# Mixture of experts behind a decayed linear attention: the building of the token lists is put in another order

## The chip, the cores and the metric

One Trainium2 chip, one of its cores. The metric is device time in microseconds (us) of one execution. The engines are named as the profile names them: PE (matrix products; PEld its weight loads), DVE (VectorE), ACT (ScalarE), POOL (GpSimd), SP (SyncE, which issues most transfers). Every engine works through its own instructions in program order and waits for other engines by semaphores.

## The reference

```python
# attention: 4 batches, 8 heads, 768 tokens, head size 64
for t in range(S):
    state = gamma * state + outer(k[t], v[t])
    y[t] = scale * q[t] @ state
x = y as (3072 tokens, 512)
# experts: 4 groups of 4, each token goes to one expert
g = argmax(x @ w_group);  e = argmax(x @ w_expert[g])
out[token] = softmax_g * softmax_e * (relu(x @ w1[g, e]) @ w2[g, e])
```

A token's expert, and the weight that its result is multiplied by, come from x, so they are known only once the attention has reached that token.

## The kernel before

**Attention.** `attention` takes 12 steps `i`, each of 128 tokens of two batches (256 tokens, `u` = 0, 1). A step on PE is: `score_mm` of the next step (L235), `state_out` (L286), `value_out` (L299), `state_mm` (L261), `logits_mm` of the step before (L319: the 20 router logits), transposes of keys (L220) and of x (L345), `select_mm` (L332). On DVE it is: `score_mask` (four instructions of L247 to each step, a pair to each `u`: pf <- sh) and `out_x` (a pair of L311: the x products, xt <- op). A matmul that reuses the bank of a score waits until L247 has read it. x goes to DRAM (`xd`), from where the experts gather their tokens.

**Lists.** Four chunks of 128 tokens are a batch (`BATCHES`, six of them). `route` is a generator; `route_steps` runs it on to its next "wait". For one batch it issues on DVE the argmaxes down to the one-hot of the expert, `oh` (L384 to L402); `weights` (six instructions L413 to L426 that end with the reciprocal `wt`, then four that split `wt` into three bf16 pieces of `pc`, L428 to L434); rank matmuls on PE (L441, L443); the sums down to the slot `sf` of each token (L451 to L460). For batches 3 to 5 (`soon`) the weights come ahead of the ranks, or right behind them for the last one. Then `spread`: `places` (three small instructions L483 to L485: tile `y` and place `p` of the slot), `entries` (on DVE the tile's marks `sel`, L503; on POOL their product with the pieces, `ent`, 128x640, L505) and `marks` (the one-hots `hot` of the place, 128x512 on DVE, L492). `tally` multiplies hot with ent on PE (L526) and adds the result to `lists` (L531). In steps 4, 6, 8 and 10 weights and `spread` stand on DVE between the two pairs of L247; `tally` is at the end of the step, in step 10 ahead of `value_out`.

**First units.** `ua` is expert 0's first 128 tokens (taken from the first 16 chunks), `ub` the rest of expert 0 (up to 108), `va` expert 1 (`us[0]`). Behind the attention `run` interleaves ua's matmuls (`layers`, L834 with hidden halves f0 to f3, then L869) with batch 5: ranks, `late_spread` (a second one-hot of the slots beyond 128, L555 on DVE, `latep` L550 on POOL), `late_ids` (L563) which gives ub's tokens, the gather of ub, the last spread and tally, the gather of va. `own_cols` gives column counts that PE loads into shape registers (`shape`, L801). `order` sorts the experts by size. hl (the low part of h, L842, for ua L1306 from a list `held`) is made on DVE.

**Weights.** Each expert's four 1 MB tiles `wf` are split in eight parts by `wsplit`: the high part on ACT (L745), the low one `wl` on DVE (L747, 128x1024). Expert 0's low parts are made on POOL beside the attention (128x512). Of va's, parts 0 and 1 stand on DVE ahead of ub's first hl, parts 2 to 5 one behind each of the four hl, and parts 6 and 7 go to POOL:

```python
if i == 7:
    for k in (6, 7):
        self.wsplit(va, k, eng=nc.gpsimd, high=False)
    self.wload(us[1], 3)
```

Then follow xbl of va's two token tiles (L812 on DVE), which va's first matmul needs. From there on the 15 units run one after another.

Of the kernel before, what the change touches and what calls it, by code (L numbers as in the profile page):

```python
# [22 lines left out]
P = 128  # L23
# [83 lines left out]
class Kernel:  # L107
# [251 lines left out]
    def route(self, i):  # L359
# [50 lines left out]
        soon = c0 + n >= EARLY  # L410

        def weights():
# [15 lines left out]
            V.tensor_copy(pc[:, :, 2], wt)  # L428
            yield 1
            V.tensor_tensor(wt, wt, pc[:, :, 2], ALU.subtract)  # L430
            yield 1
            V.tensor_copy(pc[:, :, 3], wt)
            yield 1
            V.tensor_tensor(pc[:, :, 4], wt, pc[:, :, 3], ALU.subtract)  # L434
            yield 1
# [25 lines left out]
        yield 1  # L461
        if end:
            self.late_spread()
            yield "late"
# [9 lines left out]
        if not end:  # L474
            self.spread(i)

    def places(self, b):

        c0, n = BATCHES[b]
        sf = self.sf[:, c0:c0 + n]  # L480
        p = self.rp.tile([P, BM], F32, name="place")
        y = self.rp.tile([P, BM], F32, name="tile")
        self.nc.vector.tensor_scalar(y, sf, 0.5 - P / 2, ROUND, ALU.add, ALU.add)  # L483
        self.nc.vector.tensor_scalar(y, y, ROUND, None, ALU.subtract)
        self.nc.vector.tensor_tensor(p, sf, y, ALU.subtract)  # L485
        return p, y
# [8 lines left out]
    def entries(self, b, y, eng):  # L495

        c0, n = BATCHES[b]
        buf = self.bp.tile([P, 4, P], F32, name="yT", bufs=1).rearrange("p d t -> p (d t)").bitcast(BF16)
        m = BM * NL
        ent = buf[:, 0:m * PIECES].rearrange("p (c l w) -> p c l w", c=BM, l=NL)  # L500
        sel = buf[:, m * PIECES:m * PIECES + m].rearrange("p (c l) -> p c l", c=BM)
        tb = self.rest[:, C_TB:C_TB + NL].unsqueeze(1).broadcast_to([P, BM, NL])
        self.nc.vector.tensor_tensor(sel, tb, y.unsqueeze(2).broadcast_to([P, BM, NL]), ALU.is_equal)  # L503
        pc = self.pc[:, c0:c0 + n].unsqueeze(2).broadcast_to([P, BM, NL, PIECES])
        eng.tensor_tensor(ent, sel.unsqueeze(3).broadcast_to([P, BM, NL, PIECES]), pc, ALU.mult)  # L505
        return ent

    def spread(self, b):

        p, y = self.places(b)  # L510
        ent = self.entries(b, y, self.nc.gpsimd)
        self.spreads.append((self.marks(p), ent))
# [55 lines left out]
    def own_cols(self):  # L568
# [5 lines left out]
        V.tensor_scalar(self.late_cols, f, float(LATE), None, ALU.min)  # L574
        self.own = self.rp.tile([1, 2], I32, name="ocols")
        for i, w in enumerate((P, LATE)):
            f = self.rp.tile([1, 1], F32, name="fcols%d" % i)
            V.tensor_scalar(f, nb[0:1, 1:2], float(-CAP - i * P), 1.0, ALU.add, ALU.max)
            V.tensor_scalar(self.own[:, i:i + 1], f, float(w if i else P + LATE), None, ALU.min)
# [483 lines left out]
    def attention(self, extra, beside):  # L1063
# [27 lines left out]
        for i in range(NS2):  # L1091
# [7 lines left out]
            if i:  # L1099
                if i > 2:  # L1100
                    self.outs(i)
                if i > 1:
                    scores(i + 1, 0)
                if i % 2 and not last:
                    self.select_late()
# [15 lines left out]
            if i == 10:  # L1121
                self.tally()
            beside(i, 5)
# [7 lines left out]
            self.state_copy(i)  # L1131
            beside(i, 4)
# [3 lines left out]
            if i < 2:  # L1136
                scores(i + 1, 0)
                scores(i + 1, 1)
            if last:
# [24 lines left out]
            if last:  # L1164
                self.route_steps(99)
            if i % 2:
# [5 lines left out]
            if i in (4, 6, 8):  # L1172
                self.tally()
# [19 lines left out]
    def run(self):  # L1193
        tc, nc = self.tc, self.nc
        with ExitStack() as ctx:
# [45 lines left out]
            def beside(i, place):  # L1241
# [14 lines left out]
                if place == 2:  # L1256
                    if last:
                        self.xtrans(ua, 'big', (0,), low=False)
                        self.wsplit(va, 0, low=False)
# [18 lines left out]
            self.trans_mm(last, self.yp)  # L1278
            self.wsplit(va, 1, low=False)
# [10 lines left out]
            first(2)  # L1290
            self.wsplit(va, 2, low=False)
            next(route)
            first(2)
            while next(route) != "late":
                pass
            p, y = self.places(len(BATCHES) - 1)
            ub["mt"] = self.pairs()
            self.late_ids(ub["mt"])
            ent = self.entries(len(BATCHES) - 1, y, nc.gpsimd)
            self.gather(ub)  # L1300
            for _ in route:
                pass
            self.spreads.append((self.marks(p), ent))
# [4 lines left out]
            self.own_cols()  # L1308
            for k in range(2):
                nc.scalar.activation(self.xg[1][:, k], self.one, AF.Copy, scale=0.0)  # L1310
            self.wsplit(va, 3, low=False)
            self.steps.append(self.order())
            self.route_steps(99)
            assert not self.steps
            pick(1)
            pick(2)
            for i, k in enumerate(self.first):
                if i == 0:
                    self.shape(ub, 5, 0, self.late_cols)
                if i == 1:  # L1320
# [15 lines left out]
            for i, k in enumerate(self.layers(ub)):  # L1336
                if i == 0:
                    self.counts()
                if i < 8 and i % 2:
                    self.wsplit(va, 4 + i // 2, low=False)  # L1340
                    self.wsplit(va, 2 + i // 2, high=False)
                    if i % 4 == 3:
# [88 lines left out]
```

## Time and profile before

| | |
|---|---|
| median of 3 runs | 421.93 us (420.22 to 423.2) |
| the profiled execution | 422.39 us, of which the span of its instructions 420.5 |
| busy: PE, DVE, ACT, POOL | 398.8, 301.8, 224.6, 161.0 us |
| mean granted clock of PE | 0.974 of 2.4 GHz |

Times of rows are microseconds from the span's start in the profiled execution, which is the one that sums are made against. A row of a timeline has start, length, engine, line, operation, output <- inputs, count and, in brackets, the idle time before it and what ended it.

### The profile page before, as it was taken

How to read it: one execution, taken by the hardware profiler on the slowest of the kernel's cores; microseconds unless marked ns; L12 is line 12 of the kernel's file. 1: busy time of each engine (PE TensorE's matmuls, PEld its weight loads, DVE VectorE, ACT ScalarE, POOL GpSimd, SP SyncE). 2: the span in 40 equal slices, each digit the busy share in tenths (PEclk: the TensorE clock that was granted, in tenths of full speed). 3: DMA queues.
4: the chain of work that ended last, by engine and by line, in shares of the span. 5: the costliest groups of instructions: out<-in, count | busy, mean ns of one | idle time of the engine just before them, and what ended most of it. 6: DMA issues, size and time to landing. Idle time of an engine off the chain costs nothing.

```text
span 420.5 us, 13852 instructions
## 1 busy us (share of the span) xinstructions
PE 398.8 (95%) x5805; PEld 331.5 (79%) x5837; DVE 301.8 (72%) x525; ACT 224.6 (53%) x342; POOL 161.0 (38%) x130
## 2 busy tenths in 40 slices
PE   9999979989979599999999999999999999999992
PEld 5889868868758487868788797978979879788792
DVE  4576794965799666988676877768778788697630
ACT  2335334531646066556565665766667667667620
POOL 4543647436437500622233450614405225052011
PEclk9999998996999789999999999999999999999997
DMA  7999998882875836778686978789887898888001
GB/s 264 352 320 359 348 327 282 272 284 85 270 223 182 334 125 231 252 248 263 232 258 240 301 267 288 256 296 284 296 306 279 282 327 279 295 302 294 13 35 36
DMA packets 39507, 107.13 MB, mean 255 GB/s; under 512 B 12116, under 2 KB 12244, under 8 KB 32276
## 3 DMA queue, kind: packets, MB, share of 16 engines
q1 hardware_dynamic: 29760, 93.57, 65.0%
q0 software_dynamic: 9536, 12.63, 8.8%
q8 instruction: 47, 0.77, 0.7%
q14 instruction: 16, 0.13, 0.1%
q10 hardware_dynamic: 148, 0.03, 0.1%
HBM read 94.18 MB, written 13.20 MB: 255 GB/s over the span
## 4 chain that ended last, share of the span: by engine, by line
PE 49%; issue 29%; DVE 11%; POOL 9%; POOLq 0%; ACT 0%; DVEq 0%; ACTq 0%
PE hps L834 14%; PE yps L869 6%; PE yps L916 5%; POOL out L993 5%; PE op L299 4%; PE sh L235 4%; PE yps L919 3%; POOL xg L769 3%; PE op L286 2%; DVE wl L747 2%; PE sh L345 2%; PE stp L261 2%; PE tpx L787 1%; PE sh L220 1%; PE log L332 1%
## 5 line engine op out<-in xcount | busy, mean ns | idle before, releaser
L747 DVE TENSOR_TENSOR wl<-wf,wh 128x1024 bf16<-128x1024 f32 x118 | 147.8, 1261 | 38.1 <-ACT wh L745 37.8
L745 ACT ACTIVATE wh<-wf 128x1024 f16<-128x1024 f32 (+1 forms) x136 | 133.8, 1001 | 0.0
L834 PE MATMUL hps<-xbl,wh 128*128 128x128 f16 (+16 forms) x544 | 130.1, 251 | 2.0 <-DVE xbl L812 1.4
L834 PE MATMUL hps<-xbh,wh 128*128 128x0 bf16 x544 | 127.2, 243 | 0.0
L834 PE MATMUL hps<-xbh,wl 128*128 128x0 bf16 x544 | 127.1, 243 | 0.0
L993 POOL DMA_INDIRECT out<-yo,mt x30 | 39.4, 1315 | 163.5 <-ACT yo L975 125.8
L834 PEld LDWEIGHTS <-wh 128*128 128x128 f16 x1088 | 96.0, 99 | 3.5 <-issue 2.5
L919 PEld LDWEIGHTS <-wh 128*128 128x128 f16 x768 | 47.1, 97 | 22.9
L839 ACT ACTIVATE hh<-hps 128x256 bf16<-128x256 f32 (+16 forms) x68 | 34.2, 503 | 48.1 <-PE hps L834 47.7
L769 POOL DMA_INDIRECT xg<-xd,mt x30 | 52.5, 1750 | 10.9 <-issue 2.9
L834 PEld LDWEIGHTS <-wl 128*128 128x128 bf16 x544 | 53.7, 99 | 1.2
L247 DVE TENSOR_TENSOR pf<-sh,tri 128x512 f32<-128x512 f32 x48 | 30.7, 685 | 23.1 <-PE op L299 9.7
L842 DVE SCALAR_TENSOR_TENSOR hl<-hps,hh 128x216 f16<-128x216 f32 (+15 forms) x64 | 36.8, 574 | 9.4 <-ACT hh L839 9.0
L789 ACT ACTIVATE xbh<-tpx 128x512 bf16<-128x512 f32 (+14 forms) x32 | 16.7, 523 | 46.4 <-PE tpx L787 46.4
L916 PE MATMUL yps<-wh,hh 128*128 128x512 f16 x96 | 36.4, 379 | 0.0
L916 PE MATMUL yps<-wh,hl 128*128 128x512 f16 x96 | 36.4, 379 | 0.0
L916 PE MATMUL yps<-wl,hh 128*128 128x512 bf16 x96 | 36.3, 378 | 0.0
L192 POOL TENSOR_TENSOR vs<-lv,cst 128x512 f32<-128x512 f32 x24 | 24.6, 1042 | 22.6 <-DMA lv<-qkv 10.0
L919 PEld LDWEIGHTS <-wl 128*128 128x128 bf16 x384 | 24.2, 97 | 11.4
L812 DVE TENSOR_TENSOR xbl<-tpx,xbh 128x512 f16<-128x512 f32 (+14 forms) x32 | 19.0, 597 | 18.7 <-ACT xbh L789 18.7
L919 PE MATMUL yps<-hl,wh 128*128 128x108 f16 (+11 forms) x384 | 29.1, 198 | 0.0
L919 PE MATMUL yps<-hh,wh 128*128 128x0 bf16 x384 | 26.6, 190 | 0.0
(190 smaller groups left out, 607.7 us busy)
## 6 DMA issues: line engine op xcount, KB each, us to landing
wf<-w1p SPq DMA_DIRECT2D x28, 1024.0 KB, 7.6
wf<-w2p SPq DMA_DIRECT2D x28, 1024.0 KB, 6.4
lq<-qkv SPq DMA_DIRECT2D x24, 256.0 KB, 6.0
lk<-qkv SPq DMA_DIRECT2D x24, 256.0 KB, 5.2
lv<-qkv SPq DMA_DIRECT2D x24, 256.0 KB, 5.9
xd<-xr SPq DMA_DIRECT2D x22, 256.0 KB, 4.7
wf<-w1p SPq DMA_DIRECT2D x16, 256.0 KB, 5.6
wf<-w2p SPq DMA_DIRECT2D x16, 256.0 KB, 5.1
```

The lines of the kernel that those rows point to most:

```text
L192: self.nc.gpsimd.tensor_tensor(o, v, g, ALU.mult)
L247: nc.vector.tensor_tensor(o, sc, tri, ALU.mult)
L745: nc.scalar.activation(u["wh"][i][:, cs], u["wf"][i][:, cs], AF.Copy)
L747: (eng or nc.vector).tensor_tensor(u["wl"][i][:, cs], u["wf"][i][:, cs], u["wh"][i][:, cs], ALU.subtract)
L769: nc.gpsimd.indirect_dma_start(out=xg[0:r, i, :], out_offset=None, in_=self.xd[0:n, :], in_offset=bass.IndirectOffsetOnAxis(ap=mt[0:r, i, ...
L834: nc.tensor.matmul(o, l[:, k, fs], m, start=(n == 0), stop=(n == 11), skip_group_check=True)
L839: nc.scalar.activation(hh[:, f, 0:W], hv[:, :, 0:W], AF.Relu)
L842: nc.vector.scalar_tensor_tensor(*rest)
L869: nc.tensor.matmul(ps[0:r, :], l[:, k, ts], m[k], start=(n == 0), stop=(n == 23))
L916: nc.tensor.matmul(big, h[:, k, 0:P], w[k], start=(n == 0), stop=(n == 23))
L919: nc.tensor.matmul(o, w[k][:, d * P:d * P + P], m, start=(n == 0 and d == 0), stop=(n == 23), skip_group_check=True,)
L993: s = nc.gpsimd.indirect_dma_start(out=self.out, out_offset=bass.IndirectOffsetOnAxis(ap=mt[0:r, i, 0:1].bitcast(U32), axis=0), in_=yo[0:r ...
```

## The change

- `places` goes to POOL, and is issued in `route` as soon as `sf` is; the four piece instructions behind the reciprocal go to POOL.
- `spread` is no longer called by `route`. In steps 4, 6, 8 it stands behind `out_x` (sel and hot behind the x products of the step), in step 10 behind both pairs of L247, and `tally` goes to the next step (5, 7, 9: behind the first `score_mm`), in step 10 behind `state_copy`, together with the token list and gather of ua. Batch 3's weights come behind its ranks.
- ua's transposes (`xtrans`) go from ahead of `value_out` in step 11 to behind it.
- Behind the attention: the rank matmuls of batch 5 half a hidden tile earlier; ub's gather ahead of `ent` on POOL; ua's held hl ahead of the one-hots; `late_count` alone ahead of ub's shape register, the other counts later; of `order` five steps there, the rest behind ua's second layer; the zeroing of `xg[1]` from ACT to POOL; va's high parts 4 and 5 during ua's second layer.
- va's low parts 6 and 7 on DVE, behind xbl of va; `counts` behind xbl too.

```diff
-        soon = c0 + n >= EARLY
+        soon = c0 + n >= NCH - BM
...
-            yield 1
+            G = nc.gpsimd
+            G.tensor_scalar(pc[:, :, 2], wt, 1.0, None, ALU.mult)
+            G.tensor_tensor(wt, wt, pc[:, :, 2], ALU.subtract)
+            G.tensor_scalar(pc[:, :, 3], wt, 1.0, None, ALU.mult)
+            G.tensor_tensor(pc[:, :, 4], wt, pc[:, :, 3], ALU.subtract)
...
+        self.at = self.places(i)
         if end:
             self.late_spread()
             yield "late"
...
-        if not end:
-            self.spread(i)
...
+        G = self.nc.gpsimd
+        G.tensor_scalar(y, sf, 0.5 - P / 2, ROUND, ALU.add, ALU.add)
+        G.tensor_scalar(y, y, ROUND, None, ALU.subtract)
+        G.tensor_tensor(p, sf, y, ALU.subtract)
...
+    def chosen(self, y):
...
         self.nc.vector.tensor_tensor(sel, tb, y.unsqueeze(2).broadcast_to([P, BM, NL]), ALU.is_equal)
+        return buf[:, 0:m * PIECES].rearrange("p (c l w) -> p c l w", c=BM, l=NL), sel
+
+    def entries(self, b, ent, sel):
+
         pc = self.pc[:, c0:c0 + n].unsqueeze(2).broadcast_to([P, BM, NL, PIECES])
-        eng.tensor_tensor(ent, sel.unsqueeze(3).broadcast_to([P, BM, NL, PIECES]), pc, ALU.mult)
+        self.nc.gpsimd.tensor_tensor(ent, sel.unsqueeze(3).broadcast_to([P, BM, NL, PIECES]), pc, ALU.mult)
...
-        p, y = self.places(b)
-        ent = self.entries(b, y, self.nc.gpsimd)
+        p, y = self.at
+        ent = self.entries(b, *self.chosen(y))
         self.spreads.append((self.marks(p), ent))
...
+    def late_count(self):
 
         V, nb = self.nc.vector, self.base
         self.late_cols = self.rp.tile([1, 1], I32, name="lcols")
         f = self.rp.tile([1, 1], F32, name="fcols")
         V.tensor_scalar(f, nb[0:1, 0:1], float(-P), 1.0, ALU.add, ALU.max)
         V.tensor_scalar(self.late_cols, f, float(LATE), None, ALU.min)
+    def own_counts(self):
+
+        V, nb = self.nc.vector, self.base
         self.own = self.rp.tile([1, 2], I32, name="ocols")
+        f = self.rp.tile([1, 2], F32, name="ofc")
+        tb = self.rest[0:1, C_TB + 2:C_TB + 4]
+        V.tensor_tensor(f, nb[0:1, 1:2].broadcast_to([1, 2]), tb, ALU.subtract)
+        for i, w in enumerate((P + LATE, LATE)):
+            V.tensor_scalar(self.own[:, i:i + 1], f[:, i:i + 1], 1.0, float(w), ALU.max, ALU.min)
...
                 if i > 1:
                     scores(i + 1, 0)
+                if i in (5, 7, 9):
+                    self.tally()
...
             if i == 10:
-                self.tally()
-            beside(i, 5)
+                self.spread(3)
             beside(i, 2)
...
             self.state_copy(i)
+            if i == 10:
+                self.tally()
+                beside(i, 5)
             beside(i, 4)
...
+            if i in (4, 6, 8):
+                self.spread(i // 2 - 2)
...
             if last:
                 self.route_steps(99)
+                self.spread(4)
...
-            if i in (4, 6, 8):
-                self.tally()
...
                 if place == 4 and last:
                     self.shape(ua, 4, 0, self.early_cols)
-                if place == 2:
-                    if last:
-                        self.xtrans(ua, 'big', (0,), low=False)
-                        self.wsplit(va, 0, low=False)
+                    self.xtrans(ua, 'big', (0,), low=False)
+                if place == 2 and last:
+                    self.wsplit(va, 0, low=False)
...
+            nc.gpsimd.memset(self.xg[1], 0.0)
             self.wsplit(va, 1, low=False)
             for k in range(8, 16):
...
             first(2)
             self.tally("sta")
             self.known()
-            first(2)
+            first(1)
             self.wsplit(va, 2, low=False)
             next(route)
-            first(2)
+            first(3)
             while next(route) != "late":
                 pass
-            p, y = self.places(len(BATCHES) - 1)
-            ub["mt"] = self.pairs()
-            self.late_ids(ub["mt"])
-            ent = self.entries(len(BATCHES) - 1, y, nc.gpsimd)
-            self.gather(ub)
             for _ in route:
                 pass
-            self.spreads.append((self.marks(p), ent))
+            p, y = self.at
+            ub["mt"] = self.pairs()
+            chosen = self.chosen(y)
+            self.late_ids(ub["mt"])
+            self.gather(ub)
+            ent = self.entries(len(BATCHES) - 1, *chosen)
             first(2)
             for h in self.held:
                 nc.vector.scalar_tensor_tensor(*h)
             self.held = None
-            self.own_cols()
-            for k in range(2):
-                nc.scalar.activation(self.xg[1][:, k], self.one, AF.Copy, scale=0.0)
+            self.spreads.append((self.marks(p), ent))
+            self.late_count()
             self.wsplit(va, 3, low=False)
             self.steps.append(self.order())
-            self.route_steps(99)
-            assert not self.steps
-            pick(1)
-            pick(2)
+            self.route_steps(5)
             for i, k in enumerate(self.first):
                 if i == 0:
                     self.shape(ub, 5, 0, self.late_cols)
+                    self.wsplit(va, 4, low=False)
                 if i == 1:
                     self.tally("sta")
                     fin = self.final.rearrange("p e i w -> p (e i) w")
@@ -1324,31 +1331,35 @@
                     self.nc.vector.tensor_copy(ub["mt"][:, 0, 1:2], self.final[:, 0, 1, 1:2])
                     va["mt"] = self.final[:, 1]
                     self.gather(va)
-                    for u in us[1:3]:
-                        self.listed(u)
+                    self.wsplit(va, 5, low=False)
                 if i == 2:
                     self.xtrans(ub, "tra")
+            self.route_steps(99)
+            assert not self.steps
+            pick(1)
+            pick(2)
+            for u in us[1:3]:
+                self.listed(u)
+            self.own_counts()
             for k in range(2):
                 self.wsplit(va, k, high=False)
             self.wload(us[1], 0)
             ub["wh"], ub["wl"] = ua["wh"], ua["wl"]
             self.gather(us[1])
             for i, k in enumerate(self.layers(ub)):
...
-                        self.wload(us[1], 1 + i // 4)
-                if i == 7:
-                    for k in (6, 7):
-                        self.wsplit(va, k, eng=nc.gpsimd, high=False)
-                    self.wload(us[1], 3)
+                if i in (1, 3):
+                    self.wsplit(va, 6 + i // 2, low=False)
+                if i in (1, 3, 5, 7, 13, 15):
+                    low = (1, 3, 5, 7, 13, 15).index(i) + 2
+                    self.wsplit(va, low, high=False)
+                    if low % 2:
+                        self.wload(us[1], low // 2)
                 if i in (8, 10):
                     self.xtrans(va, ("tra", "sta")[i // 2 - 4], (i // 2 - 4,))
                 if i in (9, 10):
                     self.shape(va, 0, i - 9, cols(0, i - 9))
+                if i == 11:
+                    self.counts()
             self.rp = self.rp2
             self.steps.append(self.items())
             pick(3)
```

## Rows read from the trace of the kernel before

**Rows 1.** Stretches: width; busy of PE, PEld, DVE, ACT, POOL; clock, DMA share, GB/s.

```profile
50.00:100.00 50.00, 45.57 (x951) 40.14 (x945) 35.09 (x113) 18.36 (x38) 26.68 (x25) 0.91 0.84 283
...
200.00:300.00 100.00, 100.00 (x1202) 82.85 (x1210) 73.16 (x81) 63.83 (x87) 35.01 (x21) 1.00 0.81 271
```

**Rows 2.** PE's waits, 20 to 150 us: total, times, longest.

```profile
PE yps L941 <- DVE hl L842: 3.4, 1, 3.4
PE sh L319 <- DVE pf L247: 1.9, 1, 1.9
PE log L441 <- DVE wt L426: 1.4, 1, 1.4
...
PE log L563 <- DVE hot L555: 1.3, 1, 1.3
PE yps L869 <- DVE key L598: 1.0, 1, 1.0
PE sh L345 <- DVE pf L247: 0.6, 2, 0.4
...
PE op L286 <- DVE xt L311: 0.5, 2, 0.3
```

**Rows 3.** The view of rows 1, for the three stretches with a lower clock.

```profile
64.00:68.00 4.00, 4.00 (x41) 3.75 (x43) 0.90 (x2) 3.32 (x6) 3.91 (x5) 0.57 0.73 263
94.00:102.00 8.00, 7.83 (x102) 6.84 (x103) 4.49 (x16) 0.00 (x0) 4.70 (x4) 0.57 0.44 129
142.00:150.00 8.00, 6.60 (x42) 5.64 (x40) 2.13 (x4) 2.27 (x4) 1.35 (x2) 0.57 0.78 297
```

**Rows 4.** Timeline of DVE in step 6.

```profile
60.12 0.17 DVE L428 CAST pc<-wt 128x4 bf16<-128x4 f32 x1
...
62.10 1.28 DVE L247 TENSOR_TENSOR pf<-sh,tri 128x512 f32<-128x512 f32 x2
```

**Rows 5.** Timelines of DVE, POOL and PE in steps 9 and 10.

```profile
91.11 0.24 DVE L413 TENSOR_REDUCE log<-ex 128x20 f32<-128x80 f32 x1
...
95.96 0.68 DVE L492 TENSOR_TENSOR hot<-rest,place 128x512 bf16<-128x512 f32 x1
96.56 1.28 DVE L247 TENSOR_TENSOR pf<-sh,tri 128x512 f32<-128x512 f32 x2
...
96.19 1.58 POOL L505 TENSOR_TENSOR yT<-yT,pc 128x640 bf16<-128x640 bf16 x1 [8.38 <-DVE yT L503]
...
92.44 0.20 PE L441 MATMUL log<-oh,stri 128*128 128x80 bf16 x1 [1.43 <-DVE wt L426]
...
103.18 0.64 PE L319 MATMUL sh<-xt,wr 128*32 128x256 f32 x8
```

**Rows 6.** Groups of POOL instructions, shapes apart: busy us, mean ns.

```profile
L192 POOL TENSOR_TENSOR vs<-lv,cst 128x512 f32<-128x512 f32 x24 | 24.6, 1042 | 22.6 <-DMA lv<-qkv 10.0 <-PE stp L261 9.6 <-issue 3.0
...
L550 POOL TENSOR_TENSOR latep<-pc,oh 128x8 bf16<-128x8 bf16 x1 | 0.2, 209 | 0.0
```

**Rows 7.** Timelines of DVE and POOL behind the attention.

```profile
117.59 0.17 DVE L428 CAST pc<-wt 128x4 bf16<-128x4 f32 x1
...
119.14 0.69 DVE L555 SCALAR_TENSOR_TENSOR hot<-rest,sf 128x512 bf16<-128x512 f32 x1
...
124.71 0.42 DVE L609 TENSOR_TENSOR eq<-pos,rest 128x256 f32<-128x256 f32 x1
...
127.81 0.61 DVE L812 TENSOR_TENSOR xbl<-tpx,xbh 128x432 f16<-128x432 f32 x1 [0.73 <-ACT xbh L789]
128.34 2.35 DVE L747 TENSOR_TENSOR wl<-wf,wh 128x1024 bf16<-128x1024 f32 x2
...
134.94 6.00 DVE L747 TENSOR_TENSOR wl<-wf,wh 128x1024 bf16<-128x1024 f32 x1
...
142.29 1.19 DVE L812 TENSOR_TENSOR xbl<-tpx,xbh 128x512 f16<-128x512 f32 x2
...
135.65 4.20 POOL L747 TENSOR_TENSOR wl<-wf,wh 128x1024 bf16<-128x1024 f32 x2
```

More of the change, by code (lines that the diff above doesn't have):

```diff
@@ L427, in weights @@
             yield 1
-            V.tensor_copy(pc[:, :, 2], wt)
-            yield 1
[L430 to L435, printed above, removed]
+            G = nc.gpsimd
[3 more added lines that the diff above has]
+            G.tensor_tensor(pc[:, :, 4], wt, pc[:, :, 3], ALU.subtract)
         if soon and not end:
@@ L482, in places @@
         y = self.rp.tile([P, BM], F32, name="tile")
-        self.nc.vector.tensor_scalar(y, sf, 0.5 - P / 2, ROUND, ALU.add, ALU.add)
-        self.nc.vector.tensor_scalar(y, y, ROUND, None, ALU.subtract)
-        self.nc.vector.tensor_tensor(p, sf, y, ALU.subtract)
+        G = self.nc.gpsimd
+        G.tensor_scalar(y, sf, 0.5 - P / 2, ROUND, ALU.add, ALU.add)
+        G.tensor_scalar(y, y, ROUND, None, ALU.subtract)
+        G.tensor_tensor(p, sf, y, ALU.subtract)
         return p, y
@@ L493, in marks @@
         return hot
-    def entries(self, b, y, eng):
-        c0, n = BATCHES[b]
+    def chosen(self, y):
         buf = self.bp.tile([P, 4, P], F32, name="yT", bufs=1).rearrange("p d t -> p (d t)").bitcast(BF16)
         m = BM * NL
-        ent = buf[:, 0:m * PIECES].rearrange("p (c l w) -> p c l w", c=BM, l=NL)
         sel = buf[:, m * PIECES:m * PIECES + m].rearrange("p (c l) -> p c l", c=BM)
@@ L503, in entries @@
         self.nc.vector.tensor_tensor(sel, tb, y.unsqueeze(2).broadcast_to([P, BM, NL]), ALU.is_equal)
+        return buf[:, 0:m * PIECES].rearrange("p (c l w) -> p c l w", c=BM, l=NL), sel
+    def entries(self, b, ent, sel):
+        c0, n = BATCHES[b]
         pc = self.pc[:, c0:c0 + n].unsqueeze(2).broadcast_to([P, BM, NL, PIECES])
-        eng.tensor_tensor(ent, sel.unsqueeze(3).broadcast_to([P, BM, NL, PIECES]), pc, ALU.mult)
+        self.nc.gpsimd.tensor_tensor(ent, sel.unsqueeze(3).broadcast_to([P, BM, NL, PIECES]), pc, ALU.mult)
         return ent
     def spread(self, b):
-        p, y = self.places(b)
-        ent = self.entries(b, y, self.nc.gpsimd)
+        p, y = self.at
+        ent = self.entries(b, *self.chosen(y))
         self.spreads.append((self.marks(p), ent))
@@ L566, in late_ids @@
         self.nc.vector.tensor_scalar(mt[:, 0, 0:1], self.pre, ps[:, 0:1], ps[:, 1:2], ALU.add, ALU.add)
-    def own_cols(self):
+    def late_count(self):
         V, nb = self.nc.vector, self.base
@@ L574, in own_cols @@
         V.tensor_scalar(self.late_cols, f, float(LATE), None, ALU.min)
+    def own_counts(self):
+        V, nb = self.nc.vector, self.base
         self.own = self.rp.tile([1, 2], I32, name="ocols")
[L576 to L579, printed above, removed]
+        f = self.rp.tile([1, 2], F32, name="ofc")
[3 more added lines that the diff above has]
+            V.tensor_scalar(self.own[:, i:i + 1], f[:, i:i + 1], 1.0, float(w), ALU.max, ALU.min)
     def order(self):
@@ L1336, in run @@
             for i, k in enumerate(self.layers(ub)):
[L1337 to L1342, printed above, removed]
-                        self.wload(us[1], 1 + i // 4)
-                if i == 7:
-                    for k in (6, 7):
-                        self.wsplit(va, k, eng=nc.gpsimd, high=False)
-                    self.wload(us[1], 3)
+                if i in (1, 3):
[5 more added lines that the diff above has]
+                        self.wload(us[1], low // 2)
                 if i in (8, 10):
```

## Prediction

> **What bounds the kernel now.** I read the stretches first. From 150 us on PE has no gap worth a row: between 200 and 300 us it is busy all the time at full clock, so nothing off PE is worth anything there [rows 1]. Between 50 and 100 us it is idle for 4.4 us and its clock averages 0.91 [rows 1]. So the change can only earn in the attention's second half and in the passage to the first experts. PE's waits there come next: the reader is to see that nearly all of them end on DVE [rows 2]. Last, the clock. In three stretches the mean clock is 0.57, that is partly the lower level of 1.2 GHz [rows 3], and each follows a wait of PE: the 1.9 us for pf, the 1.4 us for wt with two short ones behind it, the 3.4 us for hl [rows 2]. The waits of 1.3 and 1.0 us behind the attention have no such stretch behind them. A stretch loses its width times 0.43: 4.0 x 0.43 = 1.7 us; 8.0 x 0.43 = 3.4 us; the third 3.4 us, less about 0.4 for time in which PE had nothing to do anyway, so 3.0.
>
> **Step 6 (and 4, 8).** DVE's second pair of L247 can start where the first piece cast starts now, 60.12 instead of 62.10: 2.0 us earlier, since four piece instructions, three of places, sel and hot no longer stand ahead of it [rows 4]. PE's 1.9 us for it goes [rows 2], and with it, I take it, the lower clock behind it (1.7) [rows 3]. The transposes that waited for the same pair in steps 4 and 8 give 0.6 [rows 2]. What hides the moved work: sel and hot run behind the x products while PE does its transposes and the next `score_mm`, ahead of which nothing needs them, and `ent` ends about when PE comes to the tally. If that cover is gone the tally waits by the difference (bounds 0 to 1 us a batch; I take 0, since DVE is 2 us earlier). On POOL the pieces and `ent` stand ahead of expert 0's low parts and the next vs, which slip by the same time as the one-hots; a vs is used a whole step later, so I count nothing for it. Sum: 1.9 + 1.7 + 0.6 = **4.2**.
>
> **Steps 9 and 10.** The rank matmuls at 92.44 waited 1.43 us because batch 3's weights read the same PSUM bank [rows 5]; the weights go behind them, so they start at about 91.15. The 0.5 us for the x products go as well [rows 2], and the clock (3.4) [rows 3]. Here a new wait comes in. Sel and hot now stand behind the second pair of L247, and PE meets the tally behind `state_mm`. DVE: from the start of the weights (91.11) to the end of the first pair (97.76 as the instructions overlap) is 6.65 [rows 5]; less four pieces (0.8) and three places (0.5), less hot (0.6), plus the second pair (1.2) gives sel at 91.11 + 5.95 = 97.1, and `ent` takes 1.58 [rows 5]: 98.75. PE: from the ranks to the logits it is 103.18 - 92.44 = 10.74 [rows 5], less 3.4 of clock, 0.5 of waits and 0.35 of a tally at half clock: 6.5 from 91.15, so 97.65. The tally waits 1.1 us (bounds 0, if PE is not so fast, and 2). Sum: 1.4 + 0.5 + 3.4 - 1.1 = **4.2**. ua's gather comes at about 100 instead of 103, and its transposes later than now, so no wait there.
>
> **Batch 5 and ub's shape.** POOL's small instructions have no row of their size but one: a product of 128x8 takes 0.21, one of 128x512 takes 1.04 [rows 6]. I take 0.25, near the first, with both as bounds. On DVE the late one-hot starts 0.8 earlier (four pieces fewer: the 0.2 steps from 117.59 on) and would end at 119.0 instead of 119.83 [rows 7]. But `latep`, which the same matmul needs, is now queued on POOL behind four pieces and three places: 117.6 + 4 x 0.25 = 118.6 (the slots are ready by then), + 0.75 + 0.25 = 119.6. So ub's tokens come 0.2 earlier, and PE, whose rank matmuls no longer wait for a whole hidden tile, comes to them some 0.5 sooner and waits 1.6 instead of 1.3. Behind ua's last hidden quarter stand hl (0.35 earlier, its predecessors being done) and then hot (0.7), ahead of the count for ub's shape register, on which PE waits 1.0 now [rows 2]. So the count is 0.15 later, if hot runs freely. It may not: POOL has `ent` at about that time, behind ub's gather. The row that decides is va's low part on DVE at 134.94: 6.00 us where two others take 2.35 together, while two products of the same kind ran on POOL until 139.85 [rows 7]. DVE and POOL did not share; one stood still. I place `ent` 0.65 ahead of hot, an estimate: both follow ub's tokens, `ent` behind the issue of the gather, hot behind f3's matmuls, their ReLU and hl. Then hot waits for the other 0.9 of its 1.58 [rows 5]. I take **1.0 lost** here (bounds: 0.2 gained; 1.9 lost, if hot meets all of `ent`).
> The trace also has the same pair side by side, in step 10: hot at 95.96 takes its usual 0.68 although `ent` begins at 96.19 [rows 5]. By that alone hot loses nothing and the sum would be 0.9 better. The Trainium skill ("SBUF — State Buffer", Who interferes with whom) says that a VectorE instruction with two SBUF inputs and a GpSimd instruction that reads SBUF exclude each other, and that the one issued first keeps the port to its end; by that rule step 10's hot was safe only because it came first, and the new order would cost the 0.9, as the low part's row suggests.
>
> **From xbl of ub to va.** DVE alone sets this part: xbl of ub ends at 128.42, xbl of va at 143.48 [rows 7], 15.06 us. Taken away: low part 4 standing still, 6.00 - 1.18 = 4.8, as POOL has no product any more; `counts` (two of 0.42 and two small: 1.2) goes behind. Added ahead: the rest of `order` (three of 0.42 and a cast, 1.5; the size is that of the row at 124.71) and the own counts (0.45) [rows 7]. 15.06 - 4.8 - 1.2 + 1.95 = 11.0, a gain of **4.0** (bounds 3 and 4.8, for gaps between the remaining instructions and for the counts in the shade of others). DVE stays the limit: of the 15.06, PE waits 3.4 for hl alone [rows 2]. Low parts 6 and 7 cost DVE 2.35 behind va's xbl; they hide under va's first layer, in which DVE has only hl and the next unit's low parts to make; if that cover were gone they would cost their 2.35. The loads that take their buffer are issued behind them on SP, for parts that are split last in va. ACT's two more high parts fall where it mostly waits for PE; SP's two list loads come behind the rest of `order`, far ahead of their gathers; the zeroing on POOL replaces idle time. I count nothing for these.
> The lower clock behind the 3.4 us wait (3.0) goes with it. But PE's two waits behind the attention become about 1.6 and 2.0 us (1.3 and 1.0 now, and the changes above), as long as the 1.9 us behind which the clock fell in step 6. I put one such stretch there, at step 6's price: **-1.7** (bounds 0 and 3.4).
>
> **Sum**: 4.2 + 4.2 - 1.0 + 4.0 + 3.0 - 1.7 = 12.7 us. The profiled execution took 422.4 (the span and 1.9 around it), so 409.7; it lies 0.5 above the median, so I forecast **409.2**.
>
> **Rivals.**
> *The clock never falls again* and hot runs freely: 2.6 better, 406.6; with no tally wait in step 10 either, 405.5. For it: the waits of 1.3 and 1.0 brought no fall. Against: the new ones are longer.
> *The clock falls twice*, also behind the tally's wait in step 10 (3.4 again) and for longer behind the attention (1.7 more): 414.3. For it: in step 9 a wait of 1.4 with two short ones was enough [rows 2, 3].
> *The attention gives nothing back*: PE is faster there, but the loads of q, k and v take over as the limit. A step's transfers went at 283 GB/s with the DMA engines 0.84 busy between 50 and 100 us [rows 1]. Then 8.4 is lost: 417.6. Against: none of PE's larger waits names a transfer [rows 2].
> *Slower: POOL's small instructions have a high floor.* If each takes 1.04, as one of 128x512 does [rows 6], `latep` waits 8 of them: 6 us more on the path to ub; pieces and places delay the tallies by 1.5 us in each of three steps, 2.6 in step 10 and some 1.5 for batch 4; together 15, with 3 of clock 18 against the 12.7: 427. It decides where half an us more than 0.25 has eaten the gain, from about 0.8 an instruction on. Against: `latep` itself, 0.21 [rows 6].
>
> **How the numbers follow.** Forecast (407 to 412) 0.45; clock never falls 0.25; clock falls twice 0.15; attention gives nothing 0.09; POOL's floor 0.06. The range 404 to 416 holds the first three, with 0.15 left out. A measurement here tells about 1%, 4.2 us: faster by over 1% is under 417.7. That is the first three cases and a third of the fourth, 0.87 or so; most of the fourth, 0.07, within 1%; slower 0.06.
>
> **What the profile after would show.** PE's wait for pf at L319 gone and no clock under 1.0 between 60 and 75 us; ranks of batch 3 without wait, a wait of about 1 us at L526 for POOL's `ent` in step 10; pieces and places on POOL at 0.2 to 0.3 each; hot of batch 5 longer than 0.7 and PE waiting about 2 us at L869; va's low parts at 1.2 each and va's first matmul about 11 us behind ub's xbl. I would be wrong if small POOL instructions or the way from DVE to POOL and back cost much more than 0.25, if the clock falls where I have none, or if PE, faster in the attention, then waits for transfers.

## Result and the profile after

The changed kernel took 416.02 us in the median of 4 runs (413.99 to 416.26), the one before, run beside it, 421.78 (420.22 to 423.2): a ratio of 0.9854, 95% interval 0.9807 to 0.99, a gain of 5.8 us. 409.2 was forecast, with a range of 404 to 416. The profiled executions stand at 422.39 and 416.26 (spans 420.5 and 414.5), so 6.1 us are to be found where 12.7 were expected. Two executions far above the others are left out of every figure here: one of 458.5 us of the kernel before and one of 2235 us of the last experiment's kernel.

The stretches of [rows 3] in the profile of after, and a new one behind the attention (columns as in [rows 1]):

```profile
64.00:68.00 4.00, 4.00 (x103) 3.75 (x105) 2.60 (x6) 3.05 (x6) 3.80 (x5) 1.00 0.95 283
94.00:102.00 8.00, 5.78 (x110) 4.73 (x100) 4.67 (x15) 2.11 (x5) 6.29 (x10) 1.00 0.35 118
120.00:128.00 8.00, 5.95 (x25) 3.05 (x27) 3.35 (x14) 2.32 (x3) 2.45 (x3) 0.79 0.11 33
142.00:150.00 8.00, 8.00 (x92) 7.67 (x92) 6.48 (x10) 5.62 (x9) 1.06 (x1) 1.00 0.90 304
```

All three stretches at a lower clock are gone, and one has come: 8.0 x 0.21 = 1.7 us, the price forecast. But 94 to 102 shows PE idle for 2.2 us. PE's six longest waits from 20 to 150 us after, to be laid beside [rows 2]:

```profile
PE log L526 <- POOL yT L505: 2.8, 3, 2.2
PE yps L874 <- DVE gt L606: 2.2, 1, 2.2
PE log L563 <- POOL latep L550: 1.9, 1, 1.9
PE log L332 <- DVE lists L531: 1.8, 2, 1.0
PE hps L839 <- DVE hl L847: 1.2, 1, 1.2
PE yps L946 <- issue: 1.1, 3, 0.4
```

None of before's waits for pf or wt is left. In their place PE waits for POOL (`ent`, `latep`) and for a DVE instruction that was never in its way (L531). The starts of `value_out` in each step and of the units' first matmuls give what each passage took, in us. A step counts here from its `value_out` to that of the next, so the tally at the head of step 5 falls into "step 4":

| from, to | before | after | change | forecast |
|---|---|---|---|---|
| steps 4 and 8 | 16.67 | 18.55 | +1.9 | -0.6 |
| step 6 | 11.84 | 8.57 | -3.3 | -3.6 |
| step 9 | 12.57 | 8.21 | -4.4 | -5.3 |
| step 10 to ua | 14.33 | 15.76 | +1.4 | +1.1 |
| ua to ub | 15.05 | 18.55 | +3.5 | +2.7 |
| ub to va | 15.06 | 11.73 | -3.3 | -4.0 |
| va to us1 (clock) | 21.76 | 18.87 | -2.9 | -3.0 |

Steps 5 and 7 are equal within 0.01, and behind the start of us1 the two stay together. The rest of the sum is 0.75 us that step 4 began later (43.73 for 42.98); the kernels below that are the same program up to there began it between 42.8 and 44.1, so this is scatter. So 12.7 were forecast and 6.3 came, 6.4 less. Two things in the table are easy to miss. The lower clock of before from 94 to 102 us lies partly behind the start of its step 10 (99.09), so steps 9 and 10 belong together: -4.2 forecast, -3.0 measured. And up to ub's first matmul the two profiles are level (128.47 before, 128.39 after): all that the change gained in the attention it had lost again by then.

**Where steps 4 and 8 lost.** PE, then DVE, behind the first `score_mm` of step 5:

```profile
49.40 0.44 PE L526 MATMUL log<-yT,hot 128*128 128x160 bf16 x4 [0.35 <-POOL yT L505]
50.69 0.62 PE L332 MATMUL log<-rest,ls 128*128 128x20 f32 x4 [0.84 <-DVE lists L531]
49.12 1.29 DVE L247 TENSOR_TENSOR pf<-sh,tri 128x512 f32<-128x512 f32 x2 [0.89 <-PE sh L235]
50.32 0.31 DVE L531 TENSOR_TENSOR lists<-lists,log 128x160 f32<-128x160 f32 x1
```

The tally now stands directly ahead of `select_mm`, which writes the same PSUM tile (`log`). PE waits 0.35 for `ent`, and then 0.84 until DVE has added the tally to `lists`; but DVE has a pair of L247 to do first. The head of step 9 has the same (0.23 and 0.97). Before, the tally stood at the end of the step before.

**Step 10.** POOL:

```profile
93.23 1.16 POOL L752 TENSOR_TENSOR wl<-wf,wh 128x512 bf16<-128x512 f32 x1
94.35 2.04 POOL L192 TENSOR_TENSOR vs<-lv,cst 128x512 f32<-128x512 f32 x2
96.36 0.23 POOL L429 TENSOR_SCALAR pc<-wt 128x4 bf16<-128x4 f32 x1
...
96.96 0.54 POOL L431 TENSOR_SCALAR pc<-wt 128x4 bf16<-128x4 f32 x1
...
97.88 1.26 POOL L505 TENSOR_TENSOR yT<-yT,pc 128x640 bf16<-128x640 bf16 x1
```

`wt` is ready at 94.80, but the pieces stand behind a low part of expert 0 and the two vs of step 11, and start 1.56 later. The tally starts at 99.19, 2.21 late. Three of the four small instructions cost what was assumed (0.20 to 0.24), but they follow one another every 0.3 us; L431 took 0.54 (see the last section).

**Behind the attention.** POOL (pieces, places, `latep`, gather, `ent`), then DVE:

```profile
114.32 0.24 POOL L429 TENSOR_SCALAR pc<-wt 128x4 bf16<-128x4 f32 x1 [0.53 <-DVE wt L426]
...
116.71 0.20 POOL L550 TENSOR_TENSOR latep<-pc,oh 128x8 bf16<-128x8 bf16 x1
117.84 1.16 POOL L774 DMA_INDIRECT xg<-xd,mt  x1 [0.93 <-DVE mt L566]
119.03 1.28 POOL L505 TENSOR_TENSOR yT<-yT,pc 128x640 bf16<-128x640 bf16 x1
113.39 0.43 DVE L421 TENSOR_SCALAR u<-sms 128x4 f32<-128x4 f32 x1
...
119.33 1.53 DVE L489 TENSOR_TENSOR hot<-rest,place 128x512 bf16<-128x512 f32 x1
...
120.95 0.14 DVE L574 TENSOR_SCALAR lcols<-fcols 1x1 int32<-1x1 f32 x1
```

`latep` comes 2.4 us behind the first piece. hot takes 1.53 us instead of 0.7 and ends 0.55 behind `ent`, which began 0.3 ahead of it: the exclusion that was forecast, and 0.84 lost for the 0.9 forecast. The count for ub's shape (`lcols`) stands behind it, and PE goes on at 122.05, 2.2 us late, with the lower clock behind that.

**ub to va** went as worked out on DVE: each low part 1.20, from the end of ub's xbl (128.34) to that of va's (139.45) 11.1 us, where 11.0 was forecast. DVE, then PE:

```profile
138.84 0.61 DVE L817 TENSOR_TENSOR xbl<-tpx,xbh 128x432 f16<-128x432 f32 x1 [0.20 <-ACT xbh L794]
140.12 0.26 PE L839 MATMUL hps<-xbl,wh 128*128 128x236 f16 x1
```

But PE came to va's first matmul 0.67 behind xbl, without a wait for it: it was still in ub's second layer (L946, with the 1.1 us of gaps above for which the profile shows no releaser). So 3.3 came for 4.0, and at the end of this passage DVE was no longer the limit.

### The profile page after: what moved, and what is told of

It is laid out like the page before. It is cut to its first block, busy times and chain, and to the rows that moved or that the text cites. A ratio compares the mean times of both kernels' runs of the same rounds, so it can differ in the third digit from the quotient of the medians.

```text
span 414.5 us, 13859 instructions
## 1 busy us (share of the span) xinstructions
PE 393.6 (95%) x5805; PEld 326.3 (79%) x5837; DVE 294.2 (71%) x484; ACT 222.8 (54%) x340; POOL 164.3 (40%) x171
## 4 chain that ended last, share of the span: by engine, by line
PE 42%; issue 37%; POOL 12%; DVE 7%; ACT 1%; POOLq 0%; DVEq 0%; ACTq 0%
PE hps L839 10%; POOL out L998 6%; PE yps L874 6%; PE sh L235 4%; PE op L299 4%; POOL xg L774 3%; PE yps L921 3%; PE op L286 2%; PE sh L345 2%; PE yps L924 2%; PE stp L261 2%; DVE pf L247 1%; PE sh L220 1%; PE tpx L792 1%; PE yps L946 1%
## 5 line engine op out<-in xcount | busy, mean ns | idle before, releaser
L752 DVE TENSOR_TENSOR wl<-wf,wh 128x1024 bf16<-128x1024 f32 x120 | 145.3, 1220 | 37.7 <-ACT wh L750 31.9
L839 PE MATMUL hps<-xbl,wh 128*128 128x128 f16 (+16 forms) x544 | 128.8, 249 | 1.2 <-DVE hl L847 1.2
L774 POOL DMA_INDIRECT xg<-xd,mt x30 | 50.8, 1695 | 14.6 <-issue 5.5
L247 DVE TENSOR_TENSOR pf<-sh,tri 128x512 f32<-128x512 f32 x48 | 30.7, 685 | 26.1 <-PE op L299 10.5
```

The costliest lines, as they stand in the source:

```text
L247: nc.vector.tensor_tensor(o, sc, tri, ALU.mult)
L752: (eng or nc.vector).tensor_tensor(u["wl"][i][:, cs], u["wf"][i][:, cs], u["wh"][i][:, cs], ALU.subtract)
L774: nc.gpsimd.indirect_dma_start(out=xg[0:r, i, :], out_offset=None, in_=self.xd[0:n, :], in_offset=bass.IndirectOffsetOnAxis(ap=mt[0:r, i, ...
L839: nc.tensor.matmul(o, l[:, k, fs], m, start=(n == 0), stop=(n == 11), skip_group_check=True)
```

## Experiments

Theory 1, from these readings: the gains are real, and the new waits (deferred select, pieces behind vs, count behind hot, `latep` behind small instructions) give half of them back.

**One part alone, on the kernel before: va's last two low parts on DVE.**

```diff
-                if i == 7:
-                    for k in (6, 7):
-                        self.wsplit(va, k, eng=nc.gpsimd, high=False)
+                if i in (13, 15):
+                    self.wsplit(va, 6 + i // 15, high=False)
+                if i == 15:
                     self.wload(us[1], 3)
```

> The kernel before with one part of the change alone: low parts 6 and 7 of va on DVE behind va's xbl, and the load that takes their buffer behind them. Theory 1 (POOL's two products made DVE's low part 4 stand still, 6.00 instead of 1.2 us; the lower clock behind that wait goes too): from xbl of ub to xbl of va 15.06 - 4.8 = 10.3 us, no clock under 1.0 near 143 us, so 4.8 + 3.0 = 7.8 faster than before, about 414; that is more than the whole change gives, whose other parts then add up to a loss of some 2. Rival (the other parts of the change are a gain too, and this one less than its row says): at most 4 faster, 418 or more.

414.9 us (413.18 to 416.33), ratio 0.9886 (0.9819 to 0.9953) to before on the same chip (420.95). ub to va takes 10.7 us, and the clock behind it is full; the lower clock of the attention's steps 9 and 10 is still there. Low part 4, which took 6.00 us before, and two stretches:

```profile
133.76 1.22 DVE L747 TENSOR_TENSOR wl<-wf,wh 128x1024 bf16<-128x1024 f32 x1
```

```profile
92.00:100.00 8.00, 7.53 (x106) 6.38 (x100) 4.43 (x15) 0.00 (x0) 4.70 (x4) 0.58 0.52 157
141.00:149.00 8.00, 8.00 (x95) 7.34 (x95) 6.37 (x11) 5.99 (x8) 1.05 (x1) 1.00 0.91 298
```

This one part is worth 6.0 us, as much as the whole change; in its place the profile shows 7.2, 4.3 from ub to va (10.7 for 15.06) and 2.9 from va to us1 (18.9 for 21.76).

**The reverse: the changed kernel with these two parts back on POOL** (behind ub's fourth hl, as before).

> The changed kernel with va's low parts 6 and 7 back on POOL, behind ub's fourth hl, and nothing else undone. Theory 1 (these two parts carry the whole net gain, since what the rest of the change gains in the attention it loses again at its new waits): DVE's low part that meets them stands still for about 4.8 us again, PE waits for hl at L946 and the clock falls behind it; 416.0 + 4.8 + 1 to 3 = 421.8 to 424, that is no faster than before. Rival (the rest has a gain of its own, and the low parts' gain and the rest's only overlap, both ending on the same engine): part of it is left, 417 to 419. What is seen between the end of ub's xbl and that of va's decides: 15 to 16 us by theory 1, 11 to 13 by the rival.

417.97 us (416.0 to 420.39), ratio 0.992 (0.9878 to 0.9962). So the strict form of theory 1, no faster than before, falls; but these 3 us are not shown to be a gain that the rest of the change has of its own. DVE, then POOL, ahead of va, and the stretch behind va's start:

```profile
140.13 2.86 DVE L752 TENSOR_TENSOR wl<-wf,wh 128x1024 bf16<-128x1024 f32 x1
...
139.54 5.43 POOL L752 TENSOR_TENSOR wl<-wf,wh 128x1024 bf16<-128x1024 f32 x2
```

```profile
144.00:148.00 4.00, 3.84 (x42) 3.79 (x42) 2.67 (x6) 1.35 (x3) 3.06 (x3) 1.00 0.43 152
```

In the new order POOL's products hold only one low part, which gets in between the two: DVE loses 2.86 - 1.20 = 1.7 us, where before it lost 4.8 [rows 7], and the clock behind stays full. ub to va takes 12.5 us and va to us1 18.9. Against before that is 2.6 + 2.9 = 5.5 us gained in this place, where the low parts' move alone gained 7.2 and the whole change 6.2 (11.73 and 18.87). So the new order and the move remove largely the same loss, and their gains (3.0 and 6.0) do not add up; with the order in place the move is worth 0.8 here. Whether it is the order that makes the products hold less, or the tenths of a us at which the two engines meet, one trace does not show. The intervals are 2 to 3 us each way.

**The deferred select ahead of the tally (steps 5, 7, 9).**

```diff
-                if i in (5, 7, 9):
-                    self.tally()
                 if i % 2 and not last:
                     self.select_late()
+                if i in (5, 7, 9):
+                    self.tally()
```

> The changed kernel with the deferred select matmuls of steps 5 and 9 ahead of the tally instead of behind it. Theory 1 (select writes the same PSUM bank from which DVE must first add the tally to the lists, and that addition stands behind a pair of L247): PE's two waits at L332 (1.8 us) go, the tally's waits for POOL shrink by the 0.6 that the selects take, 1.8 to 2.2 us faster, about 414. Rival (PE only waits elsewhere, since transfers or DVE set the pace of these steps): the waits move to the next matmuls, under 0.5 faster.

414.45 us (410.51 to 415.8), ratio 0.9844 (0.9769 to 0.992). The waits at L332 are gone, and of those at L526 only step 10's is left:

```profile
PE log L526 <- POOL yT L505: 2.5, 1, 2.5
```

```profile
96.00:102.00 6.00, 4.56 (x40) 3.12 (x39) 1.74 (x5) 2.16 (x5) 4.54 (x5) 0.72 0.18 57
```

Steps 4 and 8 take 16.3 us together, for 18.55 in the changed kernel and 16.67 before. Step 9's `value_out` begins 2.0 us earlier (83.85 for 85.87, step 4's being level); in the stretch above the clock (0.72) gives 6.0 x 0.28 = 1.7 of it away, behind step 10's 2.5 us.

**The count for ub's shape ahead of places, one-hots and hl.**

```diff
+            self.late_count()
             p, y = self.at
...
             self.spreads.append((self.marks(p), ent))
-            self.late_count()
```

> The changed kernel with the count for ub's shape register made on DVE as soon as batch 5's slots are known, ahead of the held hl and of the one-hots. Theory 1 (the count stands behind a one-hot that waits 0.84 us for POOL's product; PE's 2.2 us wait for it, and the lower clock behind it, are the loss behind the attention): PE's wait at L874 under 0.3 us, no stretch of lower clock behind it, 2.2 + 1.7 = 3.9 faster, about 412. Rival (that passage is set by DVE's list work anyway, and the clock falls from the wait for latep alone): the wait goes but ub's first matmul comes at most 1 us earlier, 415.

414.97 us (413.74 to 416.06), ratio 0.9897 (0.9837 to 0.9956). The wait at L874 is gone, ua to ub takes 14.5 instead of 18.55, and no clock falls there; but it falls in step 10, which this edit does not touch:

```profile
PE log L526 <- POOL yT L505: 2.8, 2, 2.5
```

```profile
100.00:106.00 6.00, 5.64 (x64) 4.03 (x65) 2.23 (x7) 2.87 (x7) 3.85 (x4) 0.72 0.36 114
120.00:126.00 6.00, 6.00 (x45) 3.49 (x44) 4.14 (x16) 3.75 (x5) 3.21 (x3) 1.00 0.34 115
```

4.0 us gained in the place; in the time at most 1 (416.02 to 414.97), and the ratio to before, 0.9897, is no better than the changed kernel's 0.9854.

**Batch 3's spread right behind its weights in step 10, the vs of step 11 behind it.**

```diff
-            if not last:
+            if not last and i != 10:
                 self.vprep(i + 1)
...
+                if i == 10:
+                    self.spread(3)
+                    self.vprep(11)
...
-            if i == 10:
-                self.spread(3)
```

> The changed kernel with sel and hot of batch 3 right behind its weights, ahead of the second pair of L247, and vs of step 11 on POOL behind that batch's pieces and product. Theory 1 (in step 10 the pieces stood 1.6 us behind the two vs in POOL's queue, and sel behind the pair): the tally's 2.2 us wait for POOL falls to 0.5 or less, 1.7 faster, about 414.3. Rival (POOL's four small instructions and the product are themselves the time, 1.5 + 1.3 us): the wait stays above 1.5, under 0.7 faster.

416.41 us (414.78 to 420.77), ratio 0.9919 (0.987 to 0.9968): no gain. The tally's wait fell from 2.2 to 0.9, and a transfer came in its place, ua's gather:

```profile
PE tpx L792 <- DMA xg<-xd,mt: 1.9, 1, 1.9
```

```profile
97.97 2.04 POOL L192 TENSOR_TENSOR vs<-lv,cst 128x512 f32<-128x512 f32 x2
100.20 1.28 POOL L774 DMA_INDIRECT xg<-xd,mt  x1 [0.18 <-issue]
```

The gather now stood behind vs: its tokens were there at 99.13, and it went at 100.20. The order needed is spread, gather, vs, as in the kernel with all places mended below, where this wait is gone.

**`latep` made as soon as the expert's one-hot is there** (L550 ahead of pieces and places).

> The changed kernel with latep made on POOL as soon as batch 5's one-hot of the expert is there, instead of behind its four pieces and three places. Theory 1 (PE's 1.9 us wait for ub's tokens is latep's place in POOL's queue): PE waits for DVE's one-hot L555 instead and the matmul of ub's tokens runs 1.2 us earlier from ua's first matmul on; in the time under 1 us, since DVE's tokens instruction stands behind sel, which waits for POOL's tile, and the count behind that. Rival (the way from POOL to PE costs it wherever it stands): the wait stays at 1.9.

417.48 us (415.89 to 420.56), ratio 0.9944 (0.9909 to 0.9979), no gain:

```profile
PE yps L879 <- DVE gt L611: 3.1, 1, 3.1
...
PE log L568 <- POOL pc L433: 0.7, 1, 0.7
```

1.2 us less at the late matmul, 0.9 more at the shape register: PE only came sooner to what it had to wait for in any case, since the count that it waits for there came no earlier (120.93 for 120.95).

**Batch 5's one-hots ahead of the held hl**, one execution:

> The changed kernel with one part undone: batch 5's one-hots on DVE ahead of ua's held hl, as in the kernel before; they then start before POOL's product (ent). Theory 1 (DVE's instruction with two SBUF inputs and POOL's product exclude each other, the first one holding on): the one-hots take 0.69 again instead of 1.53, the count comes about 1 us earlier, and PE's wait for it at L874 falls from 2.2 to about 1.2. Rival (POOL's products slow DVE's instructions wherever they overlap, in the order does not matter): 1.0 us or more in this order too. Trace only; the time is expected 1 to 3 faster, the clock deciding.

417.03 us in its one run. DVE:

```profile
121.23 0.68 DVE L489 TENSOR_TENSOR hot<-rest,place 128x512 bf16<-128x512 f32 x1
...
123.39 0.90 DVE L596 TENSOR_TENSOR cnt<-nb,rest 128x16 f32<-128x16 f32 x1
```

hot is free again and the shape wait falls from 2.2 to 0.9 us; `ent` (122.97 to 124.25) now stops a product of 128x16 instead (0.90 for 0.15). The order of hot and `ent` sets the 0.8 us. One run says nothing of the time.

**The pieces on DVE again, everything else as changed.**

```diff
-            G = nc.gpsimd
+            G = V
             G.tensor_scalar(pc[:, :, 2], wt, 1.0, None, ALU.mult)
```

> The changed kernel with the four small piece instructions of each batch back on DVE, places staying on POOL. Theory 1 (what costs is POOL's queue, in step 10 behind two vs and behind the attention ahead of latep): the tally's wait in step 10 falls by about 1 us, latep comes 0.9 earlier; DVE's second pair of L247 comes 0.8 later in steps 4, 6 and 8, which returns about 0.7 of step 6's wait. Net 0 to 1 faster. Rival (POOL's price of 0.31 an instruction, against 0.2 on DVE, is the loss): 2 us or more faster.

425.81 us (423.51 to 427.36), ratio 1.0118 (1.007 to 1.0166): some 10 us slower than the changed kernel. Neither the theory nor the rival had that. DVE and POOL in step 6:

```profile
63.98 0.71 DVE L429 TENSOR_SCALAR pc<-wt 128x4 bf16<-128x4 f32 x1
64.73 0.96 DVE L430 TENSOR_TENSOR wt<-wt,pc 128x4 f32<-128x4 f32 x1
...
63.63 2.04 POOL L192 TENSOR_TENSOR vs<-lv,cst 128x512 f32<-128x512 f32 x2
```

The first two pieces stand still, one to the end of each vs. In before the same pieces took 0.17 [rows 4] while POOL idled: `ent` stood ahead of vs in its queue there, and now stands behind. The pair of L247 comes late, PE waits 1.9 us for it as in before and 6.6 us for `ent` in three steps together, and the clock is down in four stretches (0.57 to 0.72). So at this place of the new order the pieces cost more on DVE than on POOL.

None of the four single mendings (select, count, step 10, `latep`) is faster in time than the changed kernel beyond the intervals; what they show is in the traces. Together it is otherwise.

**All five places mended**: select ahead of tally, count first, `latep` early, spread ahead of ua's gather ahead of vs in step 10, and ub's token list ahead of `sel`.

> The changed kernel with five places in the order mended: deferred selects ahead of the tally (steps 5, 9), batch 3's one-hots ahead of the second pair of L247 in step 10 and vs of step 11 behind ua's gather, latep ahead of the pieces, the count for ub's shape ahead of the tokens, those ahead of sel. Theory 1 (each of the waits seen is the order's): none of PE's waits between 40 and 130 us over 1 us, no stretch of lower clock, against the changed kernel 1.8 + 1.3 + 3.9 + 0.6 = 7.6 faster, about 408.5. Rival (PE only moves on to waits for transfers, ua's gather among them, and the clock falls anyway): 412 or more.

408.43 us (407.38 to 410.35, 6 runs), ratio 0.9725 (0.9689 to 0.976), clear of the changed kernel's interval. PE's waits up to 150 us, and the stretch from 48 to 148:

```profile
PE sh L235 <- issue: 1.6, 3, 1.0
PE log L527 <- POOL yT L506: 0.9, 1, 0.9
```

```profile
48.00:148.00 100.00, 94.40 (x1723) 80.71 (x1722) 78.44 (x205) 48.69 (x90) 60.15 (x81) 1.00 0.83 280
```

PE waits for no engine longer than 0.9 us, and the clock is full throughout. Against after, ua to ub is 4.4 us shorter (14.18), step 4 1.4, step 10 1.3 and ub to va 0.9; in step 8 a gap of 1.04 us, for which the profile shows no releaser, hides what was gained.

**The same without `latep` early.**

> The kernel with all five places mended (408.4 us), with latep put back to where the changed kernel has it, behind four pieces and three places in POOL's queue. Theory 1 (waits behind the attention only tell once no later one covers them): here no later wait covers it, since the count of ub's shape stands early; PE waits 1.9 instead of 0.7 at the late matmul, and the time is 1.2 longer without a fall of the clock, 409.6, with one of the price of step 6 (1.7) 411.3. Rival (latep doesn't matter, as its move alone brought nothing): 408.4.

405.8 to 409.3 us in three runs, ratio 0.9665 (0.9574 to 0.9756), an interval that holds the other's. The wait at the late matmul is back (1.8 for 0.7) and ua to ub takes 16.1 instead of 14.2 us, as theory 1 has it, with the clock down once in that passage; but this execution came to ua 1.5 us earlier mostly since such gaps were smaller, so its span is only 1.1 longer. That `latep` pays in the time stays open.

## Why the prediction missed

**Right.** What bounds the kernel; that step 6's pf wait and its lower clock go (3.3 of 3.6); that batch 3's ranks stop waiting (4.4 of 5.3 in step 9); low parts of 1.2 us and 11 us from xbl to xbl; the clock behind it (2.9 of 3.0); the exclusion of hot by `ent` at its price; one lower stretch behind the attention at 1.7. Two of these are partly luck. The price of hot's wait came from two figures that were both 0.3 high (`ent` 1.28 for 1.58, its lead 0.3 for 0.65), and the row that it relied on, the low part of 6.00 us, began ahead of POOL's products and not behind them (last section). And that the clock fell once, and there, holds for this execution: the last section has the same program with other falls. No rival came as described: small POOL instructions have no floor near 1 us, and no transfer took over. By its size the third came close all the same, since the attention and the passage to ub together gained nothing; but it was PE's new waits that took the gain, not the loads.

**The step that failed** is "I take 0, since DVE is 2 us earlier", for the moved tallies: steps 4 and 8 were to give 0.6 and cost 1.9, 2.5 of the missing 6.4 us. It looked only at what the tally waits for. What stands behind it, `select_mm` on the same PSUM tile, had to wait for DVE's reading of the tally behind a pair of L247; with the select ahead these waits were gone, and steps 4 and 8 took 0.4 less than before instead of 1.9 more.

**Sized wrong.** Step 10's tally: 1.1 forecast, 2.2 measured. Counted from the ranks, PE came to it when forecast (6.5 us), and `ent` ended 1.1 us late (8.7 for 7.6). The estimate counted DVE's work and left out POOL's queue, where a low part and vs stand ahead of the pieces (1.56 us); with vs behind them the wait was 0.9. Of vs the prediction asked only who waits for it, not who stands behind it. Behind the attention: 2.7 forecast, 3.5 lost. PE's two waits there, forecast at 1.6 and 2.0, were 1.9 and 2.2; `latep` came 0.6 later behind the first piece than was worked out (2.4 for 1.75: seven instructions at 0.34 each). From ub to va 0.7 is missing because PE, and no longer DVE, ended the passage.

**Overvalued.** The profile of before that the sum was made on has a mean clock of 0.974. Runs of before beside the first experiments had 0.973 to 0.992 (417.87 us at 0.988, 423.65 at 0.973), so in many executions part of the lower clock that the change removes is not there to be removed. The kernel with the low parts alone, the same program as before up to ub, shows it for step 6: PE waits the same 1.9 us for pf, and the clock is 1.00 from 64 to 68 us, where before had 0.57. This comes on top of the 6.4 us, which lie between two profiled executions.

With its new waits mended the same change reaches 408.4 us. The prediction's figure for that is not 409.2 but the 405.5 of its first rival, without a fall, hot's wait or the tally's: 16.4 us of gains. Up to the start of us1 that kernel is 14.6 us ahead of before (150.69 for 165.29). So the gains were sized to within 2 us; the new waits were not.

## What to carry to other kernels

When a matmul group is moved, look at what stands behind it on its engine and writes the same PSUM tile: it inherits the wait for the reader. When small work moves to another engine, list that engine's queue at the new place before pricing the instructions, and ask which of the two engines will be running when they meet. An edit that removes a wait pays only if the engine does not reach the next one sooner; mend the waits of a stretch together, then measure.

## What the runs showed of the hardware

DVE and POOL shut each other out in both directions, down to 128x4: hot took 1.53 us behind `ent`; POOL's L431 took 0.54 and, in the step 10 kernel, L430 0.67 for 0.20 to 0.23 while DVE made hot; DVE's L421 took 0.43 for 0.16 during POOL's zeroing of `xg`, which only writes. The `ent` of [rows 5] was held too: 1.58 us, begun 0.23 behind hot, where 1.26 was enough with hot done (97.88 in after). The Trainium skill ("SBUF — State Buffer", Who interferes with whom) gives the rule, that the one issued first keeps the shared port to its end; the 0.68 and the 1.53 of hot agree with it.

The start that the profile shows does not always say who is first. The low part of 6.00 us on which the prediction relied began at 134.94, 0.7 ahead of POOL's products (135.65) [rows 7], and yet stood still until they ended. So did hot in the kernel with all places mended (2.46 us; the count stood ahead of it and little was lost). In both cases the product came right behind the issue of a gather that was under way when DVE began. POOL before, then DVE and POOL in the mended kernel:

```profile
134.54 1.08 POOL L769 DMA_INDIRECT xg<-xd,mt  x1 [0.31 <-PE tpx L787]
```

```profile
115.11 2.46 DVE L490 TENSOR_TENSOR hot<-rest,place 128x512 bf16<-128x512 f32 x1
...
114.53 1.16 POOL L779 DMA_INDIRECT xg<-xd,mt  x1 [0.78 <-DMA wf<-w2p]
115.72 1.28 POOL L506 TENSOR_TENSOR yT<-yT,pc 128x640 bf16<-128x640 bf16 x1
```

DVE began 0.40 and 0.58 behind the gather's start there. A gather with no product behind it did not hold a low part that began 0.40 later (133.36 and 133.76, with the low parts alone on DVE: 1.22 us), and one that began 0.19 behind a gather with a product behind it ran free (138.51 and 138.70, with them back on POOL: 1.20 us). So a product seems to take its place while the gather ahead of it is still being issued; that is inferred from these four rows, and no run tests it.

The clock did not follow from the length of a wait alone. Up to ub's second layer the changed kernel and the one with the low parts back on POOL are the same program; behind the same 2.2 us wait in step 10 the first kept full clock, and the second did not:

```profile
100.00:104.00 4.00, 2.62 (x18) 1.71 (x18) 1.74 (x5) 0.49 (x2) 2.56 (x3) 0.74 0.00 0
```

Where it fell in one such place it cost 1.7 us (8.0 x 0.21, 6.0 x 0.28): a forecast can price a fall, but these runs do not let it say in which execution one comes.
